# Second MLP: w_out's tiles behind y's second pair, the second maximum behind the turned rows, weights a slot later

## The chip, the cores and the metric

The kernel runs on one core of a Trainium2 chip. Its engines are TensorE (PE in the profile, with its weight loads as PEld), VectorE (DVE), ScalarE (ACT), GpSimd (POOL) and SyncE (SP), which here issues the DMAs. The metric is the device time of one execution in microseconds; the median of three runs stands for the kernel.

## The reference

Three stages in a row: an attention without a score matrix, an MLP, and a second MLP with a softmax and a layer norm in its middle.

```python
q_s = exp(q - max(q, -1));  q_s /= sum(q_s, -1) + 1e-9      # (8, 8, 576, 64)
k_s = exp(k - max(k, 2));   k_s /= sum(k_s, 2) + 1e-9
x = q_s @ (k_s^T @ v)                                       # as 4608 x 512
h = x @ w_in                                                # 512 -> 2048
y = (max(h, 0) + alpha * min(h, 0)) @ w_out                 # 2048 -> 512
h = y @ w_in2                                               # 512 -> 1024
e = exp(h - max(h, -1));  s = h * e / (sum(e, -1) + 1e-9)
ln = (s - mean(s)) / sqrt(var(s) + 1e-6) * g_ln
out = ln @ w_out2                                           # 1024 -> 512
```

## The kernel before

**Products.** Each 2 x 2 block product is done with seven products in place of eight (operands A11, A12, S1 to S4, A22 on one side, B11, B21, T1 to T4, B22 on the other). Each operand is split into a high and a low part (`put`, lines 132 to 134: ACT rounds to the high part, L133, and DVE subtracts it, L134), and each product is three matmuls, high by high, high by low, low by high.

**Stages.** The attention and the first MLP's first pass over nine tiles of 512 tokens (`phase(0)`) end at about 475 us; the second pass (`phase(1)`) runs to about 873 us; then the second MLP goes over 18 pairs of 128-token rows. The weights of the first MLP's second pass are fetched and split during the first pass, in eight slots a tile, from slot 4 of the third last tile on (`z = n - (NTL - 3) * SLOTS - 4`).

**One pair of the second MLP.** `load_y(n)` fetches the seven operands of y from DRAM (y_A, y_S, SP L1372). `pe_h2(n)` makes h in three parts: products into two PSUM banks h2a and h2x, ACT copies a bank that has to be kept (`hold`, r, L1397), DVE adds into hs (L1404, L1412, L1414). `norm_pieces(n, z)` is the softmax and the norm of each of the pair's two 128-token halves z: the maximum on DVE (`top`, L1446), the exponential with its sum on ACT (L1447), `solu` on DVE (L1436 to L1439), squares on ACT (L1449), the variance on DVE (L1442), its root on POOL (L1443), L1451 on DVE, and the scaled rows el on ACT (L1452). `pe_tr(n, z)` turns the rows by TensorE (tp, L1487); ACT copies them (fA, L1498), and DVE and ACT form the operands l and lS of the output product: L1510, L1513, L1515, L1518 and their `put`s; the last row is the low part of S4. `pe_out(n)` makes the output in banks oa and ox, with holds on ACT (or, L1539) and adds on DVE (L1553, L1561, L1563).

**Order.** A scheduler walks the emitted steps by priority and writes one list per engine; an engine does its list in order, and waits where an instruction's inputs aren't there. The loop over pairs emits, for pair n: `pe_h2(n+1, 0)`, `pe_tr(n, 0)`, `pe_h2(n+1, 1)`, `pe_tr(n, 1)`, `norm(n+1, 0)`, `pe_h2(n+1, 2)`, `load_y(n+2)`, `pe_out(n, 0)`, `norm(n+1, 1)`, `pe_out(n, 1)`. `tc.issue_after(x)` ties what is emitted in it behind x in its own engine's list. In pairs 1 to 7 the loop also works off what is left of y: steps `y_late`, which copy and store y's operands (yl, ACT and DVE L133, L134 and SP L529).

**w_out.** Its 14 tiles wo (512 KB each) are fetched by SP at the start of the second MLP: 8 behind y's first pair, in `first_h2`, and 6 behind y's second pair, in `second_h2`.

Of the kernel before, what the change touches and what calls it, by code (L numbers as in the profile page):

```python
# [13 lines left out]
ALU = mybir.AluOpType  # L14
# [6 lines left out]
def attention_then_two_mlps(  # L21
# [42 lines left out]
    NTL = NT // N  # L64
# [41 lines left out]
    def f32(ap):  # L106
        return ap.bitcast(F32)
# [23 lines left out]

    def put(hi, lo, src, eng=V):
        S.activation(hi, src, AF.Copy)  # L133
        eng.tensor_tensor(lo, src, f32(hi), ALU.subtract)  # L134


    wps = [tc.alloc_tile_pool(name="wp0", bufs=7 + FU, side="right")]
# [704 lines left out]
    SLOTS = 8  # L842
# [321 lines left out]
    def hook0(i, s):  # L1164
        n = i * SLOTS + s
        for what in LOADS.get(n, []):
            chunk_load(*what)
        with ExitStack() as behind:
            for ins in booted if i == 0 else ():
                behind.enter_context(tc.issue_after(ins.ins))  # L1170
            for what in READY.get(n, []):
                chunk_ready(*what)
        if (i, s) == SUMS_AT[0]:
            for o in ("S1", "S2", "S3"):
                wc[0, o] = w_tile(0, 0, o)
        if (i, s) in SUMS_AT:
            sums.pop(0)()
        if (i, s) == (TS - 1, 3):
            s4_step(0)
        if (i, s) == (TS, 0):  # L1180
            s4_step(1)
        if (i, s) == (NTL - 3, 4):
            ps_at.release()
            at.release()
            ahead.append(tc.alloc_tile_pool(name="ahead", bufs=1, reuse_waits="tile"))
        z = n - (NTL - 3) * SLOTS - 4
        if 0 <= z < len(NEXT):
            u, o = NEXT[z]
            while to_turn:
                to_turn.pop(0)()  # L1190
            raw = ahead[0].tile([P, N, 2], I32, tag="w64", name=f"a64_{u}_{o}")
            w = ahead[0].tile([P, N], I32, tag="w32", bufs=4 * FU, name=f"a32_{u}_{o}")
            out = not isinstance(o, str)
            src = src_out(1, u, o) if out else src_in(1, u, o)
            load, *turn_ = load_parts(src, raw, w, None if out else 2)
            load()
            to_turn.extend(turn_)
            second[u, o] = f32(w)
        elif z == len(NEXT):
            while to_turn:  # L1200
                to_turn.pop(0)()
        if i == NTL - 1 and s == 2:
            ready["in", 0] = w_in_ops(1, 0, {o: second[0, o] for o in ("A11", "A12", "A21", "A22")}, gp_s(0), V, V)
        if i == NTL - 1 and s in IN_AT:
            for _ in range(IN_AT[s]):
                ready["in", 0].pop(0)()
# [148 lines left out]
    def fetch_wi(o, u):  # L1355
        wi[o] = wps[u].tile([P, 2, N], F32R, tag="w", name=f"wi_{o[0]}_{o[1]}")
        nc.sync.dma_start(out=f32(wi[o]), in_=wi_d[o])

    def fetch_wo(o, pool):
        wo[o] = pool.tile([P, 2, 2, W], F32R, tag="w", bufs=None, name=f"wo_{o[0]}_{o[1]}")  # L1360
        nc.sync.dma_start(out=f32(wo[o]), in_=wo_d[o])
# [3 lines left out]
    def load_y(n):  # L1365


        i, z = divmod(n, 2)
        ys[n] = {}
        for o in STAT:  # L1370
            ys[n][o] = m2["pool"].tile([P, 2, 2, P], F32R, tag=f"y{o}", bufs=1, name=f"y_{n}_{o}")
            asked = nc.sync.dma_start(out=f32(ys[n][o]), in_=y_d[i][STAT.index(o)][:, z])  # L1372
        return asked
# [47 lines left out]
    def norm(n, z):  # L1421
        for piece in norm_pieces(n, z):
            piece()

    def norm_pieces(n, z):
        t = 2 * n + z
        h = hs[n][z]
        st = m2["pool"].tile([P, 8], F32, tag="st", bufs=4, name=f"st_{t}")
        nm, se, rs, su, sq, rstd = (st[:, z:z + 1] for z in range(6))
        if t == 0:  # L1430
            m2["pool"].tile([P, 3 * SHIFT], F32, name="l_edge")
        e = m2["pool"].tile([P, F2], F32, tag="el", bufs=2, name=f"el_{t}")
        lns[t] = e

        def solu():
            V.tensor_scalar_add(se, se, 1e-9)  # L1436
            V.reciprocal(rs, se)
            V.scalar_tensor_tensor(e, h, rs, e, ALU.mult, ALU.mult, accum_out=su)  # L1438
            V.tensor_scalar_mul(su, su, -1.0 / F2)  # L1439

        def spread():
            V.tensor_scalar(sq, sq, 1.0 / F2, 1e-6, ALU.mult, ALU.add)  # L1442
            G.tensor_tensor(rstd, sq, mhalf, ALU.pow)  # L1443

        return [
            lambda: V.tensor_reduce(nm, h, AX.X, ALU.max, negate=True),  # L1446
            lambda: S.activation(e, h, AF.Exp, bias=nm, accum_out=se),  # L1447
            solu,
            lambda: S.activation(h, e, AF.Square, bias=su, accum_out=sq),  # L1449
            spread,  # L1450
            lambda: V.tensor_tensor(su, su, rstd, ALU.mult),  # L1451
            lambda: S.activation(e, e, AF.Identity, bias=su, scale=rstd),  # L1452
        ]
# [18 lines left out]

    def lt_put(n, o, src):
        t = lt_op(n, o)
        put(t[:, 0], t[:, 1], src)

    lf = {}

# [12 lines left out]
    def pe_tr(n, z):  # L1491


        tps = turned_rows(n, z)

        def copy(o, src):
            lf[n, o] = m2["pool"].tile([P, 4, P], F32, tag=f"f{o}", bufs=1, name=f"f{o}_{n}")
            S.activation(lf[n, o], src, AF.Copy)  # L1498

        if z == 0:  # L1500
            copy("A11", tps[0])
            lt_put(n, "A11", tps[0])
            copy("A12", tps[1])
            lt_put(n, "A12", tps[1])
        else:
            copy("A22", tps[1])
            f11, f12, f22 = (lf.pop((n, o)) for o in ("A11", "A12", "A22"))
            t = gp.tile([P, 2, N], F32, tag="rn", bufs=1, name=f"fs_{n}")
            s, s3 = (t[:, y, :].rearrange("p (f q) -> p f q", f=4) for y in range(2))
            V.tensor_tensor(s, tps[0], f22, ALU.add)  # L1510
            a21 = tps[0]
            lt_put(n, "A22", tps[1])
            V.tensor_tensor(s3, f11, a21, ALU.subtract)  # L1513
            lt_put(n, "S1", s)
            V.tensor_tensor(s, s, f11, ALU.subtract)  # L1515
            lt_put(n, "S2", s)
            lt_put(n, "S3", s3)
            V.tensor_tensor(f12, f12, s, ALU.subtract)  # L1518
            lt_put(n, "S4", f12)

    ob = {}

# [87 lines left out]
    def hook1(i, s):  # L1610
        if i == 0:
            hook_w1(i, s)
        if i == 1 and s == 0:
            open_w2()
        if i and s in (4, 5, 6, 0) and y_todo:
            y_todo.pop(0)()
        for step in prep.get((i, s), []):
            step()
        if i == NTL - 1:
            if s in (2, 3):  # L1620
                for o in late[:7][4 * (s - 2):4 * (s - 1)]:
                    fetch_wi(o, 0)
            if s == 7:
                for o in late[7:]:
                    fetch_wi(o, 1)

    def first_h2():
        while y_todo:
            y_todo.pop(0)()
        wr["pool"].release()  # L1630
        xp.release()
        m2["pool"] = tc.alloc_tile_pool(name="m2", bufs=1, reuse_waits="tile")
        m2["pool"].tile([P, STEP], F32, name="y_edge")
        ps_g.release()
        psum["h2"] = tc.alloc_tile_pool(name="ps_h2", bufs=2, space=PSUM, reuse_waits="tile")
        asked = load_y(0)
        m2["w"] = tc.alloc_tile_pool(name="m2w", bufs=2, reuse_waits="tile")
        m2["w"].tile([P, SHIFT], F32, name="w_edge")
        with tc.issue_after(asked.ins):
            for z in range(8):  # L1640
                fetch_wo(WO[z], wps[z // 4])

    def second_h2():
        for z in range(3):
            pe_h2(0, z)
        load_y(1)
        norm(0, 0)
        for z in range(8, 14):
            fetch_wo(WO[z], wps[1] if z < 12 else m2["w"])

    phase(1, [first_h2, second_h2], hook1)
    norm(0, 1)
# [9 lines left out]
    for n in range(NPR - 2):  # L1662
        at_end = pe_h2(n + 1, 0)
        with ExitStack() as behind:
            if n == 0:
                behind.enter_context(tc.issue_after(at_end.ins))
            pe_tr(n, 0)
        if n:
            store_y(asked)
        if n and y_late:  # L1670
            y_late.pop(0)()
        pe_h2(n + 1, 1)
        pe_tr(n, 1)
        norm(n + 1, 0)
        pe_h2(n + 1, 2)
        asked = load_y(n + 2)
        store_y(asked)
        pe_out(n, 0)
        norm(n + 1, 1)
        if n and y_late:  # L1680
            y_late.pop(0)()
        if n < NPR - 3:
            pe_out(n, 1)
# [144 lines left out]
```

## Time and profile before

| | us |
|---|---|
| median of three runs | 1285.52 |
| the three runs | 1282.73 to 1285.69 |
| the profiled execution | 1283.44 |
| its span in the trace | 1281.7 |
| PE busy | 1242.3 (97%) |
| DVE busy | 1009.2 (79%) |
| ACT busy | 792.6 (62%) |

The granted TensorE clock was 0.999 of full speed (2.4 GHz) over the span. A row of the timeline reads: start, duration, engine, line, operation, out <- in, and in brackets the engine's idle time before it with what released it. A busy PE is counted from modelled ends, so the windows below are read by their length first.

### The profile page before, as it was taken

To read this page: it belongs to the slowest core of one execution; us is meant where nothing else is said; L and a number is where in the kernel's file an instruction comes from. 1 tells how busy PE (TensorE), PEld (TensorE's weight loads), DVE (VectorE), ACT (ScalarE), POOL (GpSimd) and SP (SyncE) were. 2 spreads that over 40 slices of the span, in tenths; PEclk is the share of its full clock that TensorE was granted. 3 is DMA by queue.
4 is the path that set the end of the run, shared out by engine and by line. 5 is a ranking of instruction groups with operands and counts; after the bars stand their busy time and mean duration, and the time that the engine had idled before them with its cause. 6 is when DMAs were issued, how large, how long until landed. Compare 5 with 4: busy or idle time off the path is not lost.

```text
span 1281.7 us, 22036 instructions
## 1 busy us (share of the span) xinstructions
PE 1242.3 (97%) x8443; PEld 1109.2 (87%) x8443; DVE 1009.2 (79%) x1818; ACT 792.6 (62%) x1371; POOL 27.0 (2%) x52
## 2 busy tenths in 40 slices
PE   4899999999999999999999999999999999999998
PEld 3788888898988889998998999997888888898988
DVE  7899987988866687887889888864777778686865
ACT  5776554654655565654566555544777677777774
POOL 0100000000000000000000000000000000000000
PEclk9999999999999999999999999999999999999999
DMA  9964553454424430534665557579434345334312
GB/s 242 286 175 137 144 151 105 120 172 104 141 72 146 142 139 33 210 127 177 243 230 209 202 197 263 190 243 379 148 119 150 118 134 154 115 109 112 111 59 50
DMA packets 153401, 203.83 MB, mean 159 GB/s; under 512 B 57144, under 2 KB 105296, under 8 KB 150096
## 3 DMA queue, kind: packets, MB, share of 16 engines
q1 hardware_dynamic: 152208, 201.38, 48.8%
q0 software_dynamic: 1088, 1.05, 0.5%
q8 instruction: 66, 1.08, 0.4%
q14 instruction: 39, 0.32, 0.1%
HBM read 126.37 MB, written 76.02 MB: 158 GB/s over the span
## 4 chain that ended last, share of the span: by engine, by line
PE 77%; DMA 8%; DVE 8%; ACT 5%; issue 1%; SPq 1%; POOL 0%; ACTq 0%; DVEq 0%; POOLq 0%
PE acc L471 8%; PE acc L472 8%; PE acc L473 8%; PE ga L361 4%; PE ga L362 4%; PE ga L363 4%; PE gx L361 3%; PE gx L363 3%; PE gx L362 3%; PE oa L1533 2%; PE tp L1487 2%; PE h2a L1390 2%; PE h2a L1392 2%; PE h2a L1391 2%; PE oa L1534 2%; PE oa L1535 2%
## 5 line engine op out<-in xcount | busy, mean ns | idle before, releaser
L471 PE MATMUL acc<-gg,w 128*128 128x512 f32 x576 | 226.0, 392 | 0.9 <-ACT w L212 0.9
L472 PE MATMUL acc<-gg,w 128*128 128x512 f32 x576 | 226.7, 394 | 0.0
L473 PE MATMUL acc<-gg,w 128*128 128x512 f32 x576 | 224.3, 391 | 0.0
L473 PEld LDWEIGHTS acc<-gg,w 128*128 128x128 f32 x576 | 108.1, 188 | 23.3 <-DVE w L213 0.3
L471 PEld LDWEIGHTS acc<-gg,w 128*128 128x128 f32 x576 | 108.2, 188 | 20.3 <-ACT w L212 1.0
L472 PEld LDWEIGHTS acc<-gg,w 128*128 128x128 f32 x576 | 108.2, 188 | 17.9 <-DVE gg L134 0.3
L134 DVE TENSOR_TENSOR gg<-t,gg 128x1024 fp32r<-128x1024 f32 x72 | 88.0, 1222 | 14.5 <-ACT gg L133 14.4
L133 ACT ACTIVATE gg<-t 128x1024 fp32r<-128x1024 f32 x72 | 76.5, 1063 | 30.0 <-DVE t L452 20.7
L452 DVE SCALAR_TENSOR_TENSOR t<-rn,calpha,t 128x512 f32<-128x512 f32 x120 | 84.7, 748 | 9.2 <-ACT rn L449 9.2
L449 ACT ACTIVATE rn<-t 128x1024 f32<-128x1024 f32 x60 | 63.2, 1053 | 32.4 <-DVE t L438 32.3
L134 DVE TENSOR_TENSOR l<-tp,l 128x512 fp32r<-128x512 f32 x50 | 34.3, 685 | 46.6 <-ACT l L133 46.6
L361 PE MATMUL ga<-xT,w_S 128*128 128x256 f32 x240 | 68.3, 285 | 1.3 <-ACT r L370 1.3
L363 PE MATMUL ga<-xT,w_S 128*128 128x256 f32 x240 | 67.0, 279 | 0.0
L362 PE MATMUL ga<-xT,w_S 128*128 128x256 f32 x240 | 67.0, 279 | 0.0
L370 ACT ACTIVATE r<-ga 128x512 f32<-128x512 f32 x60 | 35.7, 594 | 41.1 <-PE ga L363 40.9
L1452 ACT ACTIVATE el<-el,st 128x1024 f32<-128x1024 f32 x36 | 44.5, 1242 | 21.2 <-DVE st L1451 10.0
L389 PE MATMUL h<-xB,w_c 128*128 128x256 f32 x192 | 54.9, 288 | 1.4 <-ACT w_c L212 1.3
L391 PE MATMUL h<-xB,w_c 128*128 128x256 f32 x192 | 54.7, 285 | 1.1 <-DVE w_c L213 1.0
L390 PE MATMUL h<-xB,w_c 128*128 128x256 f32 x192 | 54.4, 284 | 0.0
L1498 ACT ACTIVATE fA<-tp 128x512 f32<-128x512 f32 x50 | 30.1, 603 | 30.1 <-PE tp L1487 30.1
L361 PEld LDWEIGHTS ga<-xT,w_S 128*128 128x128 f32 x240 | 45.1, 188 | 4.1 <-ACT r L370 2.3
L1438 DVE SCALAR_TENSOR_TENSOR el<-hs,st,el 128x1024 f32<-128x1024 f32 x36 | 46.2, 1282 | 0.6
(399 smaller groups left out, 3990.8 us busy)
## 6 DMA issues: line engine op xcount, KB each, us to landing
y_S<-y_d SPq DMA_DIRECT2D x72, 256.0 KB, 3.0
xraw<-x_d SPq DMA_DIRECT2D x16, 1024.0 KB, 4.9
y_d<-yo_S SPq DMA_DIRECT2D x32, 512.0 KB, 3.5
y_A<-y_d SPq DMA_DIRECT2D x54, 256.0 KB, 2.7
y_d<-yo_A SPq DMA_DIRECT2D x24, 512.0 KB, 2.9
p_d<-pt SPq DMA_DIRECT2D x36, 256.0 KB, 3.5
part<-p_d SPq DMA_DIRECT2D x9, 1024.0 KB, 8.3
q<-in_q_dram SPq DMA_DIRECT2D x16, 512.0 KB, 5.5
```

The source lines that it names most:

```text
L133: S.activation(hi, src, AF.Copy)
L134: eng.tensor_tensor(lo, src, f32(hi), ALU.subtract)
L361: T.matmul(bank[:, z, :], wh, x[:, 0, c, :], start=first and z == 0, stop=False, **go_on)
L362: T.matmul(bank[:, z, :], wh, x[:, 1, c, :], start=False, stop=False, **go_on)
L363: T.matmul(bank[:, z, :], wl, x[:, 0, c, :], start=False, stop=c == 1, **go_on)
L389: T.matmul(out, w[:, 0, c, :], x[:, 0, c % 2, :], start=c == 0 and h == 0, stop=False, **go_on)
L391: T.matmul(out, w[:, 1, c, :], x[:, 0, c % 2, :], start=False, stop=c == KC - 1, **go_on)
L449: S.activation(rn, t, AF.Relu, scale=-1.0)
L452: V.scalar_tensor_tensor(t[:, j, :], rn[:, j, :], calpha[:, fg + j:fg + j + 1], t[:, j, :], ALU.mult, ALU.add)
L471: T.matmul(a, wh, g[:, 0, :], start=u == 0 and f == 0, stop=False)
L472: T.matmul(a, wh, g[:, 1, :], start=False, stop=False)
L473: T.matmul(a, wl, g[:, 0, :], start=False, stop=u == NU - 1 and f == FU - 1)
```

## The change

Four edits. The last maximum of a pair (`top` of `norm(n+1, 1)`) is tied on DVE behind the last row of `pe_tr(n, 1)`, for which `put`, `lt_put` and `pe_tr` return it. Of the wo tiles, 2 are fetched at slot 7 of the last tile of the first MLP, 2 behind y's first pair, and 10 behind y's second pair. The weights of the first MLP's second pass are fetched one slot later, and their pools are released one slot later.

```diff
-        if (i, s) == (NTL - 3, 4):
+        if (i, s) == (NTL - 3, 5):
             ps_at.release()
...
-        z = n - (NTL - 3) * SLOTS - 4
+        z = n - (NTL - 3) * SLOTS - 5
...
             if s == 7:
                 for o in late[7:]:
                     fetch_wi(o, 1)
+                for z in range(2):
+                    fetch_wo(WO[z], wps[0])
...
         with tc.issue_after(asked.ins):
-            for z in range(8):
-                fetch_wo(WO[z], wps[z // 4])
+            for z in range(2, 4):
+                fetch_wo(WO[z], wps[0])
...
-        load_y(1)
+        asked = load_y(1)
         norm(0, 0)
-        for z in range(8, 14):
-            fetch_wo(WO[z], wps[1] if z < 12 else m2["w"])
+        with tc.issue_after(asked.ins):
+            for z in range(4, 14):
+                fetch_wo(WO[z], wps[1] if z < 12 else m2["w"])
...
-        pe_tr(n, 1)
+        turned_all = pe_tr(n, 1)
...
-        norm(n + 1, 1)
+        top, *others = norm_pieces(n + 1, 1)
+        with tc.issue_after(turned_all.ins):
+            top()
+        for piece in others:
+            piece()
```

The first place is DVE's list in pair 9. hs_0 and st_12039 belong to the first half of pair 10, hs_1 and st_12132 to its second half, lS and l are operands of pair 9, and L1446 is the second maximum. Before:

```order
L1446 TENSOR_REDUCE st_12132<-hs_1_11943 128x1
L1515 TENSOR_TENSOR fs_12020<-fs_12020,fA_9_11985 128x512
L134 TENSOR_TENSOR lS_9_12033<-fs_12020,lS_9_12033 128x512
L1518 TENSOR_TENSOR fA_9_11990<-fA_9_11990,fs_12020 128x512
L1437 RECIPROCAL st_12039<-st_12039 128x1
L1553 TENSOR_TENSOR ob_9_12075<-ox_12074,or_9_12089 128x256
L134 TENSOR_TENSOR lS_9_12030<-fs_12020,lS_9_12030 128x512
L1438 SCALAR_TENSOR_TENSOR el_12040,st_12039<-hs_0_11942,st_12039,el_12040 128x1024
L134 TENSOR_TENSOR l_9_12022<-fA_9_11990,l_9_12022 128x512
L1439 TENSOR_SCALAR st_12039<-st_12039 128x1
L1436 TENSOR_SCALAR st_12132<-st_12132 128x1
```

The same place now:

```order
L1518 TENSOR_TENSOR fA_9_11990<-fA_9_11990,fs_12020 128x512
L134 TENSOR_TENSOR lS_9_12030<-fs_12020,lS_9_12030 128x512
L1437 RECIPROCAL st_12039<-st_12039 128x1
L1553 TENSOR_TENSOR ob_9_12075<-ox_12074,or_9_12089 128x256
L134 TENSOR_TENSOR l_9_12022<-fA_9_11990,l_9_12022 128x512
L1438 SCALAR_TENSOR_TENSOR el_12040,st_12039<-hs_0_11942,st_12039,el_12040 128x1024
L1446 TENSOR_REDUCE st_12132<-hs_1_11943 128x1
L1439 TENSOR_SCALAR st_12039<-st_12039 128x1
L1561 TENSOR_TENSOR ob_9_12076<-oa_12073,or_9_12130 128x256
L1436 TENSOR_SCALAR st_12132<-st_12132 128x1
L1437 RECIPROCAL st_12132<-st_12132 128x1
L1438 SCALAR_TENSOR_TENSOR el_12133,st_12132<-hs_1_11943,st_12132,el_12133 128x1024
```

The second maximum went from in front of L1515 to behind S4's low part (l_9 <- fA_9) and behind L1438 of the first half; the second half's L1436, L1437 and L1438 follow it, and the low part of S4 stands in front of the first L1438 now.

The second place is ACT's list in the same pair, from the holds of the output on. el_12040 is the first half of pair 10, el_12133 the second, r_11 are the holds of pair 11. Before:

```order
L1539 ACTIVATE or_9_12116<-oa_12073 128x256
L1449 ACTIVATE hs_0_11942,st_12039<-el_12040,st_12039 128x1024
L1539 ACTIVATE or_9_12130<-ox_12074 128x256
L1452 ACTIVATE el_12040<-el_12040,st_12039 128x1024
L1449 ACTIVATE hs_1_11943,st_12132<-el_12133,st_12132 128x1024
L1566 ACTIVATE ob_9_12076<-oa_12073 128x256
L1452 ACTIVATE el_12133<-el_12133,st_12132 128x1024
L1397 ACTIVATE r_11_12211<-h2a_12186 128x512
L1397 ACTIVATE r_11_12219<-h2x_12187 128x512
```

The same stretch now:

```order
L1539 ACTIVATE or_9_12116<-oa_12073 128x256
L1539 ACTIVATE or_9_12130<-ox_12074 128x256
L1447 ACTIVATE el_12133,st_12132<-hs_1_11943,st_12132 128x1024
L1449 ACTIVATE hs_0_11942,st_12039<-el_12040,st_12039 128x1024
L1452 ACTIVATE el_12040<-el_12040,st_12039 128x1024
L1449 ACTIVATE hs_1_11943,st_12132<-el_12133,st_12132 128x1024
L1566 ACTIVATE ob_9_12076<-oa_12073 128x256
L1397 ACTIVATE r_11_12211<-h2a_12186 128x512
L1452 ACTIVATE el_12133<-el_12133,st_12132 128x1024
L1397 ACTIVATE r_11_12219<-h2x_12187 128x512
```

The second exponential (L1447, in front of this stretch before) stands behind the holds of the output, and one of the two holds r moved in front of the second L1452.

The third place is PE's list in the second pair's h, at the start of the second MLP; h2a and h2x are the two banks, wi_T_1_9187 the end of the operand T2, wi_T_0_9189 and wi_T_1_9191 are T1, wi_T_0_9225 and wi_T_1_9227 T3, and tp the first pair's turned rows. Before:

```order
L1392 MATMUL h2a_9652<-wi_T_1_9187,y_S_9571 128x512
L1390 MATMUL h2x_9653<-wi_T_0_9189,y_S_9573 128x512
L1391 MATMUL h2x_9653<-wi_T_0_9189,y_S_9573 128x512
L1392 MATMUL h2x_9653<-wi_T_0_9189,y_S_9573 128x512
L1390 MATMUL h2x_9653<-wi_T_1_9191,y_S_9573 128x512
L1391 MATMUL h2x_9653<-wi_T_1_9191,y_S_9573 128x512
L1392 MATMUL h2x_9653<-wi_T_1_9191,y_S_9573 128x512
L1487 MATMUL tp_0_0_9687<-ident,el_9583 128x128 x4
L1487 MATMUL tp_0_1_9692<-ident,el_9583 128x128 x4
L1390 MATMUL h2a_9652<-wi_T_0_9225,y_S_9575 128x512
```

The same place now:

```order
L1392 MATMUL h2a_9652<-wi_T_1_9187,y_S_9563 128x512
L1390 MATMUL h2a_9652<-wi_T_0_9225,y_S_9567 128x512
L1391 MATMUL h2a_9652<-wi_T_0_9225,y_S_9567 128x512
L1392 MATMUL h2a_9652<-wi_T_0_9225,y_S_9567 128x512
L1390 MATMUL h2a_9652<-wi_T_1_9227,y_S_9567 128x512
L1390 MATMUL h2x_9653<-wi_T_0_9189,y_S_9565 128x512
```

T3's product into h2a comes right behind T2's now, where the products with T1 into h2x and eight transposes stood between; the hold r of bank h2a (ACT, L1397) lies between the two.

## Rows read from the trace of the kernel before

**Rows 1.** The page: busy us (share of the span) xinstructions.
```profile
PE   1242.3 (97%) x8443; PEld 1109.2 (87%) x8443; DVE 1009.2 (79%) x1818; ACT 792.6 (62%) x1371; POOL 27.0 (2%) x52
```

**Rows 2.** Waits of PE, 840 to 1282 us: total us, times, longest us.
```profile
PE oa L1533 <- ACT lS L133: 3.5, 7, 1.3
PE h2a L1390 <- ACT r L1397: 2.3, 1, 2.3
...
PE h2a L1390 <- DMA y_A<-y_d: 0.6, 1, 0.6
```

**Rows 3.** Windows of 8 and 7 pairs: length, engines' busy us, clock, DMA share, GB/s.
```profile
902.51:1079.87 177.36, 173.56 (x1138) 154.72 (x1137) 133.29 (x286) 129.38 (x238) 8.77 (x16) 1.00 0.43 134
1079.87:1230.39 150.52, 150.52 (x995) 135.62 (x994) 109.48 (x232) 108.77 (x197) 7.68 (x14) 1.00 0.36 111
```

**Rows 4.** Timeline of DVE in one late pair (pair 9): start, duration.
```profile
1140.42 0.69 DVE L134 TENSOR_TENSOR l<-tp,l 128x512 fp32r<-128x512 f32 x1 [3.32 <-ACT l L133]
...
1144.16 0.68 DVE L1510 TENSOR_TENSOR fs<-tp,fA 128x512 f32<-128x512 f32 x1
...
1146.75 1.21 DVE L1446 TENSOR_REDUCE st<-hs 128x1 f32<-128x1024 f32 x1
1147.88 0.68 DVE L1515 TENSOR_TENSOR fs<-fs,fA 128x512 f32<-128x512 f32 x1
...
1151.88 0.69 DVE L134 TENSOR_TENSOR l<-fA,l 128x512 fp32r<-128x512 f32 x1
1152.48 0.15 DVE L1439 TENSOR_SCALAR st<-st 128x1 f32<-128x1 f32 x1
1152.54 0.15 DVE L1436 TENSOR_SCALAR st<-st 128x1 f32<-128x1 f32 x1
...
1154.14 0.15 DVE L1442 TENSOR_SCALAR st<-st 128x1 f32<-128x1 f32 x1
...
1161.90 0.69 DVE L134 TENSOR_TENSOR l<-tp,l 128x512 fp32r<-128x512 f32 x1 [3.31 <-ACT l L133]
```

**Rows 5.** Timeline of ACT in the same pair.
```profile
1143.17 0.60 ACT L1498 ACTIVATE fA<-tp 128x512 f32<-128x512 f32 x1 [1.81 <-PE tp L1487]
...
1148.00 1.16 ACT L1447 ACTIVATE el<-hs,st 128x1024 f32<-128x1024 f32 x1 [0.68 <-DVE st L1446]
1149.06 0.18 ACT L1447 ACTIVATION_READ_ACCUMULATOR el<-hs,st 128x1 f32 x1
...
1155.20 1.24 ACT L1452 ACTIVATE el<-el,st 128x1024 f32<-128x1024 f32 x1 [1.02 <-DVE st L1439]
...
1158.68 1.25 ACT L1452 ACTIVATE el<-el,st 128x1024 f32<-128x1024 f32 x1 [0.84 <-DVE st L1451]
...
1160.31 0.59 ACT L1397 ACTIVATE r<-h2x 128x512 f32<-128x512 f32 x1
1160.79 0.60 ACT L1498 ACTIVATE fA<-tp 128x512 f32<-128x512 f32 x1
```

**Rows 6.** Timeline of ACT in an early pair (pair 4).
```profile
995.65 0.42 ACT L133 ACTIVATE yl_A<-part 128x256 fp32r<-128x256 f32 x1 [1.98 <-DMA y_d<-yl_S]
995.97 1.13 ACT L1447 ACTIVATE el<-hs,st 128x1024 f32<-128x1024 f32 x1
```

**Rows 7.** Timeline of PE in the same pair.
```profile
997.77 0.38 PE L1533 MATMUL oa<-wo_T,lS 128*128 128x256 f32 x1 [1.34 <-ACT lS L133]
```

**Rows 8.** The chain of waits, 865 to 895 us: start, us, what.
```profile
883.91 5.26 DMA y_S<-y_d
...
893.17 0.49 ACT r L1397
...
893.71 0.50 PE h2a L1390
```

**Rows 9.** Waits of PE, 395 to 476 us.
```profile
PE ga L361 <- ACT r L370: 1.3, 4, 0.4
PE ga L361 <- DVE t L436: 1.0, 1, 1.0
```

More of the change, by code (lines that the diff above doesn't have):

```diff
@@ L133, in put @@
         S.activation(hi, src, AF.Copy)
-        eng.tensor_tensor(lo, src, f32(hi), ALU.subtract)
+        return eng.tensor_tensor(lo, src, f32(hi), ALU.subtract)
     wps = [tc.alloc_tile_pool(name="wp0", bufs=7 + FU, side="right")]
@@ L1474, in lt_put @@
         t = lt_op(n, o)
-        put(t[:, 0], t[:, 1], src)
+        return put(t[:, 0], t[:, 1], src)
     lf = {}
@@ L1518, in pe_tr @@
             V.tensor_tensor(f12, f12, s, ALU.subtract)
-            lt_put(n, "S4", f12)
+            return lt_put(n, "S4", f12)
     ob = {}
```

## The prediction, on record before the changed kernel ran

> **What bounds the kernel now.** I read the page first: PE is busy for 97% of the span [rows 1], so a change pays only by what it does to PE's few waits, or by making PE wait elsewhere. Then the waits of PE in the second MLP: 3.5 us in seven waits of an output product for the high part of lS, 2.3 us in one wait for a hold of the second pair's h, and 0.6 us for the first y [rows 2]. Two windows, cut at the starts of the first output product of a pair, show where they lie: eight early pairs take 177.36 us, or 22.17 each, and seven late pairs 150.52 us, or 21.50 each, in which PE is busy for the whole window [rows 3]. So 21.50 is PE's own pace, and the early pairs hold (22.17 - 21.50) x 8 = 5.4 us more than that. The granted clock is 1.00 in both windows, so nothing of this is the clock.
>
> The reader is to look next at how DVE and ACT go through a late pair, since nothing in the sum is as important. DVE begins a pair with the low part of l at 1140.42, behind an idle time, and the next pair with the same step at 1161.90, 21.48 us later [rows 4]. In between the rows form a loop that closes: DVE's list up to 1151.88, the first half's L1452 on ACT at 1155.20, the second half's at 1158.68, fA at 1160.79 [rows 5], and DVE again. PE shows no wait there, yet the loop is as long as PE's pace: the cover for anything that lengthens it is small, and it is used up pair after pair.
>
> **The second maximum in the late pairs.** I set the loop's start to 0 and go through the new list. Before, DVE's list up to the end of the first half's L1438 takes 1151.88 - 1140.42 = 11.46. The maximum leaves that stretch (1147.88 - 1146.75 = 1.13) and S4's low part enters it (1152.48 - 1151.88 = 0.60): 10.93 [rows 4]. Behind it now comes the maximum, whose result is there 1.21 later, at 12.14. The exponential began 0.04 behind the maximum's end (1146.75 + 1.21 = 1147.96, 1148.00) and its sum was there 1.24 later (1149.06 + 0.18) [rows 4, 5]: 13.42. From the second half's L1436 to the first half's L1442 behind it took 1154.14 - 1152.54 = 1.60 on DVE; with 0.04 of latency that is 15.06, where before it was 1154.14 - 1140.42 = 13.72. From that L1442 over POOL to the first L1452 on ACT took 1155.20 - 1154.14 = 1.06: 16.12. From the first L1452 to the second took 3.48: 19.60. From there to fA took 2.11 with two holds r in between; one of them now stands in front of the L1452, in the time in which ACT waits for POOL anyway, so 2.11 - 0.48 = 1.63 (the hold at 1160.31, fA at 1160.79): 21.23. To the next low part took 1161.90 - 1160.79 = 1.11: **22.34, against 21.48 before, or 0.86 us more a pair.**
>
> Not every pair has this list. In every third pair (3, 6, 10, 13) the first half's L1438 stands in front of S4's and S2's low parts, and the first L1452 no longer waits for the second half's L1438; there only the exponential's end, 13.42 on ACT, is in front of it. By the same steps the second L1452 then comes about 0.5 earlier than before, and with the hold gone the loop is about 1.0 shorter, 20.5. Two such loops of 22.34 and one of 20.5 are 65.2 per three pairs, 21.73 each, if the short one makes good what the long ones lost; if PE's pace keeps it from that, a long pair costs its whole 0.86. So a late pair costs between 0.25 and 0.86; I take 0.5, near the middle, because a short pair can give back only what PE lets it. Eight pairs: **+4.0**, from 0 (some slack that the rows don't show) to 6.9 (8 x 0.86).
>
> **The second maximum in the early pairs.** The wait of 1.34 us in pair 4 [rows 7] comes from ACT's list: a step of yl waits 1.98 us for a store until 995.65, and behind it stand the exponential at 995.97 and only then the high part of lS [rows 6]. In the new list the exponential stands behind lS, and S2's high part in front of the first yl, so this wait goes. At first sight that is worth the whole 5.4 us. But the pair then has the loop of the late pairs, between 21.73 and 22.34, with the middle at 22.0, and the second yl step stands between the first half's L1449 and L1452, inside the loop; its place on ACT is 995.97 - 995.65 = 0.32 us, and its store may be late as that of the row was. I take 0.3 for it: 22.3 a pair against 22.17, **+1.0 us** over eight pairs. The ends: -5.4, if PE goes at its own pace, and +4, if half a microsecond of the store's wait falls into every pair.
>
> Here a rule of the Trainium skill speaks for the change. The page "Perfetto Trace Analysis", section "Optimization Strategy", says to look for the gaps of the most contended engine, to see which engine's update ends them, and to let that one finish sooner. By this rule alone the sum of the steady loop would be -5.4. The rows agree that the gap is there and who ends it; what they show besides is that the same two engines close a loop that is as long as PE's pace, so the update can come sooner in one place only by coming later in another.
>
> **The start of the second MLP.** The hold that PE waits for at 893.71 stands at the end of a chain through y's loads: a load of y_S takes 5.26 us from 883.91 on [rows 8]. Those loads of the second pair stood behind eight wo tiles in SP's list and stand behind four now, so they land earlier by up to four tiles' time. I let the 2.3 and the 0.6 us [rows 2] go: -2.9. A new wait takes their place: T3's product into h2a comes directly behind T2's, and between them lies the hold. From the hold's start to PE's start it took 893.71 - 893.17 = 0.54 [rows 8], and PE's pipeline ends a little behind the issue of the next matmul, so at least 0.6; with one row of ACT of 1.24 in front of the hold (as long as an L1452 [rows 5]) it would be 1.9. In pair 0 there is one more: the bank ox must be read by L1553 before the first product with S1 may write it. From fA's start over L1510 to where the maximum stood it took 1146.75 - 1143.17 = 3.6 in the late pair [rows 4, 5], and the new list of PE has some 2.0 us of products between; 1.6 us. I take 0.7 for the first and nothing for the second, since that pair's share of the lS wait goes at the same time (at most 1.3 [rows 2]). **-2.2**, from -2.9 to +0.6. For the ten tiles behind y's second pair I count nothing: that pair lands by 889.2 (883.91 + 5.26) or sooner and the first output product begins at 902.51 [rows 3, 8], so some 13 us cover them; a tile that still lands too late would cost a wait of up to a load's 5 us.
>
> **The weights a slot later.** This moves ACT and DVE rows and DMAs by an eighth of a tile in the last three tiles of the first pass, where PE's waits are 1.3 us for ACT's r and 1.0 us for DVE's t [rows 9]. They may go, or as many may come in another slot. Zero, from -2.3 to +2.3. What `put` returns adds no instruction.
>
> **The sum.** -2.2 + 1.0 + 4.0 + 0 = +2.8. The startup's extra wait in pair 0 may add its 1.6 less 1.3; I add 0.4 and come to +3.2. The profiled execution took 1283.44, so the changed one would take 1286.6; the median of the runs is 2.1 above the profiled execution, which gives 1288.7, and I write **1289 us**, 0.27% slower. What a measurement of this kernel can tell from no change is about 0.3%, 3.9 us, so this forecast lies just inside.
>
> **The rivals.** First, faster: the lS waits go, and the lengthened loop is absorbed because PE's consumers of l and el have slack that the rows of a late pair, in which nothing waits, don't show. Then early pairs fall to 21.50, late ones stay: -5.4 - 2.2 = -7.6, or 1278. For it speaks that late pairs show PE without a wait; against it that slack is used once, not eight times. It decides if a late pair's ACT list still ends in front of PE's turn. The rule cited above would give this result. Second, not slower and not faster: the loop's lengthening is only the 0.25 of the lower bound and the early pairs gain it back (21.8 against 22.17, -3.0, and +2.0 late): -3.2 with the start, within the bound at 1282.3. Third, clearly slower: the second yl step waits in front of the first half's L1452 in every early pair, as the 1.98 us of pair 4 [rows 6] did elsewhere: +4 early, +6.9 late, -1 at the start, +9.9, or 1295. It decides from the store's landing on: if a store lands later than 16 us into the loop, the first L1452 is late by the rest. That the change does not do what it says is excluded by the lists: the maximum stands behind S4's low part in every pair of them.
>
> **How the numbers follow.** The forecast (loop longer by about half a microsecond, +1 to +7) has 0.55, the first rival 0.20, the second 0.13, the third 0.12. Of the forecast's 0.55, 0.25 lie within 0.3% and 0.30 above. The first rival gives 0.17 faster and 0.03 the same, the second 0.03 and 0.10, the third is slower. Faster 0.20, the same 0.38, slower 0.42. The forecast's own range is 1286.5 to 1292.5; to leave out no more than 2 in 10 it has to take in half of the first rival and half of the third: 1281 to 1295.5.
>
> **What would show it.** A late pair of the changed kernel above 21.50 us between the starts of its first output product, with a wait of PE for DVE's or ACT's step of the loop, in two pairs out of three, shows the main term right; late pairs of 21.50 show it wrong. In the early pairs the wait of the output product for lS should be nearly gone; if the period is under 21.8 there, the loop has more slack than I count. At the start the wait of 2.3 us should be gone, and a shorter one for r should stand at T3's first product. The prediction falls if the late pairs keep PE's pace, or if a wait for a store in front of L1452 stands in the early pairs.

## The result and the profile after

The changed kernel took 1295.29 us (median of six runs, 1292.02 to 1296.40), the kernel before on the same chip 1285.38. The ratio is 1.0074, with an interval of 1.0058 to 1.0091: the change makes the kernel slower by 0.74%, or 9.9 us. The forecast was slower by 3.5; the time lies just inside the range's upper end of 1295.5, where the third rival stood.

The waits of PE in the second MLP of the changed kernel (840 to 1295 us: total us, times, longest us) answer to [rows 2]:

```profile
PE tp L1487 <- DVE l L134: 3.9, 13, 0.6
PE h2x L1390 <- DVE hs L1404: 3.0, 3, 2.1
PE ox L1533 <- DVE ob L1553: 2.1, 1, 2.1
PE h2a L1390 <- ACT r L1397: 0.7, 1, 0.7
```

The waits for lS (3.5 us) are gone, and the wait for the hold r has gone from 2.3 to 0.7 us. In their place PE waits 13 times for a low part of l before it may turn the second half's rows (before 2 times, 0.6 us), a wait for L1553 stands in pair 0, and there are three waits for L1404, the longest, 2.11 us, in the last pair of the table below (before one, 0.4 us). The windows, cut at the same starts of an output product as [rows 3], show the pairs (length, then busy us of PE, PEld, DVE, ACT, POOL, clock, DMA share, GB/s):

```profile
902.92:1086.21 183.29, 177.04 (x1145) 154.16 (x1144) 135.26 (x289) 133.51 (x241) 9.52 (x16) 1.00 0.44 141
1086.21:1241.95 155.74, 153.91 (x995) 133.97 (x994) 109.81 (x232) 110.10 (x196) 7.70 (x14) 1.00 0.36 107
```

The seven late pairs take 22.25 us each instead of 21.50, at the same granted clock of 1.00 and with the same number of DVE rows (232). The table puts the whole second MLP together for the two profiled executions. The first column's mark is one matmul near the end of the first MLP (847.65 in before, 851.30 after); the starts of a pair's first output product cut the rest.

| us | mark to pair 0 | pair 0 | pairs 1-7 | pairs 8-14 | pair 15 | end |
|---|---|---|---|---|---|---|
| before | 54.86 | 22.22 | 155.14 | 150.52 | 24.87 | 26.44 |
| after | 51.62 | 26.07 | 157.22 | 155.74 | 26.27 | 26.38 |
| difference | -3.24 | +3.85 | +2.08 | +5.22 | +1.40 | -0.06 |

The sum is +9.25, close to the 9.9 of the medians. The profiled executions differ by 12.9 us of span; the other 3.65 lie ahead of the mark. Two versions below have the same program there and their marks differ by 3.1 us, so 3.65 us there is about what two executions of one program differ by; that the change has no part in it is not shown by these two profiles alone, and the third experiment bears on it.

The loop of the prediction can be checked step by step in a late pair with the long list, the turn of pair 11. (Pairs are counted here by their first output products, from 0; by this count the pair of [rows 4, 5], called pair 9 there, is also pair 11.) First DVE, start and duration:

```profile
1149.09 0.69 DVE L134 TENSOR_TENSOR l<-tp,l 128x512 fp32r<-128x512 f32 x1 [2.83 <-ACT l L133]
...
1158.80 1.28 DVE L1438 SCALAR_TENSOR_TENSOR el<-hs,st,el 128x1024 f32<-128x1024 f32 x1
...
1160.01 1.22 DVE L1446 TENSOR_REDUCE st<-hs 128x1 f32<-128x1024 f32 x1
...
1163.04 1.28 DVE L1438 SCALAR_TENSOR_TENSOR el<-hs,st,el 128x1024 f32<-128x1024 f32 x1
...
1164.25 0.15 DVE L1442 TENSOR_SCALAR st<-st 128x1 f32<-128x1 f32 x1
...
1171.53 0.69 DVE L134 TENSOR_TENSOR l<-tp,l 128x512 fp32r<-128x512 f32 x1 [2.83 <-ACT l L133]
```

Then ACT in the same pair:

```profile
1161.32 1.16 ACT L1447 ACTIVATE el<-hs,st 128x1024 f32<-128x1024 f32 x1
...
1165.32 1.25 ACT L1452 ACTIVATE el<-el,st 128x1024 f32<-128x1024 f32 x1 [1.62 <-DVE st L1439]
...
1168.80 1.25 ACT L1452 ACTIVATE el<-el,st 128x1024 f32<-128x1024 f32 x1 [0.35 <-DVE st L1451]
...
1170.42 0.59 ACT L1498 ACTIVATE fA<-tp 128x512 f32<-128x512 f32 x1
```

Counted from 1149.09, the maximum is there at 12.14 (predicted 12.14), L1442 begins at 15.16 (15.06), the first L1452 at 16.23 (16.12), the second at 19.71 (19.60), fA at 21.33 (21.23), and the loop closes at 22.44 (22.34). Against [rows 4, 5] every step behind the maximum is late. Where PE feels it is the next row of the loop:

```profile
1150.30 0.68 DVE L134 TENSOR_TENSOR l<-tp,l 128x512 fp32r<-128x512 f32 x1
...
1151.13 0.63 PE L1487 MATMUL tp<-ident,el 128*128 128x128 f32 x4 [0.31 <-DVE l L134]
```

PE may write the second half's turned rows only when the low part has read the bank, 1150.30 + 0.68; the wait that is shown is only 0.31 of the pair's loss. The starts show more. Now, around the second half's transposes:

```profile
1150.22 0.60 PE L1487 MATMUL tp<-ident,el 128*128 128x128 f32 x4
...
1151.51 0.48 PE L1390 MATMUL h2a<-wi_T,y_A 128*128 128x512 f32 x1
```

The same place before:

```profile
1142.10 1.03 PE L1487 MATMUL tp<-ident,el 128*128 128x128 f32 x8
1142.89 0.49 PE L1390 MATMUL h2a<-wi_T,y_A 128*128 128x512 f32 x1
```

From the transposes to the next product it takes 1.29 us, before 0.79. PE counts as busy in part of it (153.91 in the window, 150.52 before), since its matmuls' ends are modelled.

### The profile page after: what moved, and what is told of

The parts are those of the page before. It is cut to its first block, busy times and chain, and to the rows that moved or that the text cites. A ratio compares the mean times of both kernels' runs of the same rounds, so it can differ in the third digit from the quotient of the medians.

```text
span 1294.6 us, 22041 instructions
## 1 busy us (share of the span) xinstructions
PE 1248.9 (96%) x8443; PEld 1107.4 (86%) x8443; DVE 1009.6 (78%) x1818; ACT 796.4 (62%) x1371; POOL 27.8 (2%) x52
## 4 chain that ended last, share of the span: by engine, by line
PE 67%; DVE 15%; ACT 8%; DMA 6%; issue 2%; POOL 1%; SPq 0%; ACTq 0%; DVEq 0%; POOLq 0%
PE acc L471 8%; PE acc L472 8%; PE acc L473 8%; PE ga L361 3%; PE ga L363 3%; PE ga L362 3%; PE gx L361 3%; PE gx L363 2%; PE gx L362 2%; ACT el L1452 2%; PE oa L1533 2%; PE h L391 2%; PE h L389 2%; PE h L390 2%; PE oa L1535 2%
## 5 line engine op out<-in xcount | busy, mean ns | idle before, releaser
L1452 ACT ACTIVATE el<-el,st 128x1024 f32<-128x1024 f32 x36 | 44.7, 1243 | 26.0 <-DVE st L1439 15.4
L1438 DVE SCALAR_TENSOR_TENSOR el<-hs,st,el 128x1024 f32<-128x1024 f32 x36 | 46.2, 1282 | 0.7
L1443 POOL TENSOR_TENSOR st<-st,mhalf 128x1 f32<-128x1 f32 x36 | 20.5, 570 | 1216.0 <-DVE st L1442 1216.0
```

## The experiments

In all of them the kernel before ran on the same chip; a ratio is against it, and the line numbers of a version may be a few off. A first set takes the edits one by one.

**The tie alone.** Of the change's diff only the lines of `put`, `lt_put`, `pe_tr` and `top`.

> Only the tie of the second maximum; w_out's loads and the weights' slot as before. Theory (the tie lengthens the loop of DVE and ACT): the late pairs take 22.2 us instead of 21.50 (+0.75 x 8 = +6), pairs 1 to 7 together about +2, the start as before with PE's wait of 2.3 us for the hold, the stretch to 873 us as before; together +7 to +8.5 us. Rival (the late pairs are longer because of what the moved w_out loads or the moved weights do to memory or to the buffers): late pairs stay at 21.50 and the whole is within 2 us of before.

Measured: 1295.05 us, ratio 1.0083 (1.0070 to 1.0097). Its windows:

```profile
902.86:1082.74 179.88, 175.35 (x1137) 153.27 (x1136) 133.23 (x286) 131.86 (x238) 8.99 (x16) 1.00 0.43 132
1082.74:1238.49 155.75, 153.97 (x995) 134.05 (x994) 109.75 (x232) 110.06 (x196) 7.67 (x14) 1.00 0.35 107
```

Late pairs 155.75, to 0.01 us as in the changed kernel (155.74). This stretch hardly scatters: in four executions without the tie (the kernel before, the next two versions, and the one without the hold below) it takes 150.45 to 150.52. The tie explains the late pairs wholly, and by itself costs as much as the whole change. Pair 0 takes 23.40, 1.2 more than before, pairs 1 to 7 1.3 more (less than that stretch scatters by, as the third run shows), and the last pair 2.0 more. The total was expected 2 to 4 us lower; what was missed are pair 0 and the last pair.

**w_out's loads alone.** Of the diff only `hook1`, `first_h2` and `second_h2`.

> Only w_out's loads moved. Theory: the second MLP's first output product comes 3 us sooner, because y's second pair lands sooner; the late pairs stay at 21.50, and pair 0 has no wait of 2 us for L1553, since four products of h stand in front of the first product with S1 here; -2 to -3 us. Rival (the wait for L1553 in pair 0 comes from the moved loads by themselves): pair 0 takes 26 us here too, and the whole is 0 to +1 us.

Measured: 1286.08 us, ratio 1.0016 (1.0007 to 1.0024), slower by 2 us: a miss. From the mark to pair 0 it takes 51.64, 3.2 us less (expected 3), but pair 0 takes 25.06 (before 22.22). PE's waits in its early pairs (902 to 1082 us):

```profile
PE oa L1533 <- ACT lS L133: 4.6, 7, 1.8
PE ox L1533 <- DVE ob L1553: 1.6, 1, 1.6
PE h2a L1390 <- DMA y_A<-y_d: 0.5, 1, 0.5
```

So the wait for L1553 in pair 0 comes with the loads, and the tie is not needed for it: the rival was right in this, though it put the whole at 0 to +1 us. Start and pair 0 together come to -0.4; the rest of the 2 us is not placed. Pairs 1 to 7 take 156.26 here, but that stretch scatters, as the next run shows. The late pairs stay at 150.45.

**The weights alone, a slot later.** Of the diff only the two lines with `NTL - 3`.

> Only the first MLP's weights a slot later. Theory: PE's waits between 395 and 476 us grow by 2 us as they did in the changed kernel (0.8 for L428, more for r), nothing else moves: +1.5 to +2.5 us. Rival (the 2 us there are the scatter between two executions): within 0.7 us of before in that stretch.

Measured: 1285.14 us, ratio 1.0006 (0.9997 to 1.0015), no difference. PE's waits from 395 to 476 us are

```profile
PE ga L361 <- ACT r L370: 0.9, 2, 0.6
PE ga L361 <- DVE t L436: 0.7, 1, 0.7
PE gx L361 <- DVE t L428: 0.4, 2, 0.3
```

2.0 us in all, where [rows 9] have 2.3 and the changed kernel had 3.7. The rival holds: what is seen there in one execution is scatter.

The same profile shows another scatter. Its engines' lists in pairs 1 to 7 are those of the kernel before, yet these pairs take 157.81 us instead of 155.14, and more than in the changed kernel (157.22). In pair 4 the yl step waits longer for its store, and PE after it:

```profile
997.96 0.42 ACT L133 ACTIVATE yl_A<-part 128x256 fp32r<-128x256 f32 x1 [3.10 <-DMA y_d<-yl_S]
```

[rows 6] have 1.98 us for it.

A second set asks whether the loop of DVE and ACT is the cause of the long pairs. From pair 9 on a row of the loop is left out, with the tie and without it. These three versions ran once each, and their late windows are read from the trace.

```diff
-            hb[n].append(hold(bx, 5))
+            hb[n].append(hold(bx, 5) if n < 9 else hb[n][2])
```

**The tie, without the hold r5.**

> The tie alone, and from pair 9 on the hold r5 of bank h2x (the last hold in front of fA on ACT, 0.48 us) is left out; the kept hold r2 is read in its place, so a part of h is not computed. Theory (the late pairs are bound by the loop through this ACT row): the late pairs go from 22.2 to 21.75 us. Rival (they are bound by something that is not on this loop, such as the turned rows' bank or the loads): they stay at 22.2.

Measured in the late window:

```profile
1085.28:1238.81 153.53, 151.58 (x995) 134.53 (x994) 109.71 (x232) 107.31 (x190) 7.67 (x14) 1.00 0.36 109
```

21.93 us a pair, 0.32 less than with the tie alone. The direction is the theory's, and "stays at 22.2" is out. The mean was expected at 21.75. From low part to low part a long list falls from 22.4 to 21.9, the whole 0.48; but without the hold every late pair gets the long list, and the short one (21.9 with the hold) no longer occurs.

**The kernel before, without the hold r5.**

> The kernel before without the hold r5 of bank h2x from pair 9 on (the kept hold r2 is read in its place, so a part of h is not computed). Theory (without the tie the late pairs are bound by PE): late pairs stay at 21.50. Rival (they are bound by the loop over DVE and ACT even before): they fall by up to 0.48.

Measured: the late window is 150.51, as before (150.52). Without the tie the same row of ACT is worth nothing: PE is the bound.

**The tie, with one maximum for both halves.**

```diff
+        one_max = z == 1 and 9 <= n < NPR - 2
+        if one_max:
+            nm = firsts[n]
...
-            lambda: V.tensor_reduce(nm, h, AX.X, ALU.max, negate=True),
+            (lambda: None) if one_max else lambda: V.tensor_reduce(nm, h, AX.X, ALU.max, negate=True),
```

> The tie alone, and from pair 9 on the second half's maximum is left out (the first half's is used for both, which leaves the function of the exponential but not its shift). Theory (what costs is the place of this one DVE row in the loop): late pairs go back from 22.2 to PE's 21.5. Rival (the cost is that S2's and S4's low parts come sooner and collide with other rows): they stay above 22.

Measured in the late window:

```profile
1082.02:1232.29 150.27, 150.27 (x996) 135.42 (x995) 103.08 (x225) 109.76 (x197) 7.67 (x14) 1.00 0.37 111
```

Seven DVE rows fewer (225 against 232), one in each pair, and the pairs are at PE's pace again, 21.47. In this kernel nothing is tied in the late pairs any more, and S2's and S4's low parts also stand elsewhere, so it shows that the maximum in its new place is needed for the loss, and not that every part of the 0.75 is its 1.13 us.

A third set goes after the early pairs' 5.4 us by another way than the change.

**yl behind S2's high part.** No maximum is moved. The pair's first yl step, whose wait for a store stood in front of lS [rows 6, 7], is tied behind S2's high part on ACT.

```diff
-        if n and y_late:
-            y_late.pop(0)()
         pe_h2(n + 1, 1)
-        pe_tr(n, 1)
+        high = pe_tr(n, 1)
+        if n and y_late:
+            with tc.issue_after(high.ins):
+                y_late.pop(0)()
```

> The kernel before, with one change: in pairs 1 to 7 the first step of yl is tied on ACT behind the high part of S2, so that its wait for a store (1.98 us in pair 4 of before) no longer stands in front of lS. Theory (the early pairs' 5.4 us come from that ACT row, not from the maximum): the waits of the output product for lS in pairs 1 to 7 are gone, the pairs take 21.6 us instead of 22.1 and the whole is 2 to 4 us faster. Rival (the early pairs are bound by the added DVE and ACT work of yl itself, wherever it stands): pairs 1 to 7 stay at 22.1, within 1 us of before.

Measured: 1283.01 us, ratio 0.9986 (0.9973 to 0.9999), 1.9 us faster where 2 to 4 were expected. Pairs 1 to 7 take 152.89 instead of 155.14, below the four executions without the tie and with this step in its old place (154.58 to 157.81); five of the seven take 21.44 to 21.55. Its waits of PE in the early pairs:

```profile
PE oa L1535 <- DVE ob L1563: 1.2, 2, 0.8
PE oa L1535 <- ACT lS L133: 0.6, 1, 0.6
```

The waits for lS are down to one, in pair 0. What keeps two pairs long is a new one, for an output add.

**The same with w_out's loads moved.**

> The same, with w_out's loads moved as in the changed kernel. Theory (the start's gain of 3 us is lost again in pair 0, because PE gets ahead of a first pair whose norm is not ready sooner): first output product 3 us sooner, pair 0 at 25 us, whole within 1 us of the run without the moved loads. Rival (the gain was lost to the yl steps that follow): 2 us faster than without the moved loads.

Measured: 1281.41 us, ratio 0.9973 (0.9959 to 0.9987), 1.6 us below the run without the moved loads, but the two intervals overlap. By the traces mark to pair 0 is 51.42 (53.71 without) and pair 0 is 25.04 (22.23): the start's gain is given back in pair 0, as the theory says, to within 0.6 us. The medians stand between the theory's 1 us and the rival's 2; what they differ by is open.

**The second yl step behind the output's add.** In the trace of that run PE waits 1.44 us for L1563 in pair 2; this add is L1561 of the kernel before, since the lines here lie two further on. DVE in front of it:

```profile
960.06 0.43 DVE L134 TENSOR_TENSOR yl_S<-part,yl_S 128x256 fp32r<-128x256 f32 x1 [1.62 <-ACT yl_S L133]
960.40 0.15 DVE L1452 TENSOR_TENSOR st<-st 128x1 f32<-128x1 f32 x1
960.47 0.15 DVE L1440 TENSOR_SCALAR st<-st 128x1 f32<-128x1 f32 x1
960.54 0.41 DVE L1563 TENSOR_TENSOR ob<-oa,or 128x256 f32<-128x256 f32 x1
```

DVE stands idle for 1.62 us in front of yl's low part. The step goes behind the add that comes next (L1565 here, L1563 before), and so behind this one too:

```diff
-        if n and y_late:
-            y_late.pop(0)()
         if n < NPR - 3:
-            pe_out(n, 1)
+            added = pe_out(n, 1)
+        if n and y_late:
+            with tc.issue_after(added.ins):
+                y_late.pop(0)()
```

> The kernel with the first yl step behind S2 and w_out's loads moved, and the pair's second yl step tied on DVE behind the output's add L1563 (here L1565). Theory (the two waits of PE for that add, 1.4 and 0.3 us in pairs 2 and 6, come from the yl rows in front of it): both go, pairs 2 and 6 take 21.6 instead of 23.5 and 22.4, whole 1.5 to 3 us faster than without this tie, about 1279. Rival (the early pairs that are long are those in which a store lands late): pairs 2 and 6 stay long.

Measured: 1280.12 us, ratio 0.9970 (0.9959 to 0.9981). The 1.5 to 3 us against the version in front of it don't show in the medians (0.9973 there, on another chip); they show in the traces. Every pair from 1 to 14 takes 21.46 to 21.59, and pairs 1 to 7 take 150.77 together, 2.7 us less than in the version in front of it and 4.4 us less than before. Its windows:

```profile
899.62:1075.49 175.87, 173.82 (x1145) 155.91 (x1144) 135.48 (x290) 131.54 (x242) 9.94 (x16) 1.00 0.45 142
1075.49:1226.02 150.53, 150.53 (x995) 135.60 (x994) 109.43 (x232) 108.78 (x197) 7.70 (x14) 1.00 0.39 119
```

This version beats both kernels. What is left over PE's pace in its first window lies in pair 0 (25.10), where PE waits 1.3 us for a load of y (y_A) and 0.7 us for L1555, the L1553 of the kernel before; the load's wait is not followed further here.

**Pair 0's L1438 behind the first add.** The next pair's L1438 is emitted behind `pe_out(0, 0)` and tied behind its first add.

> The same, and in pair 0 the next pair's L1438 is tied behind the output's first add L1553 (here L1555). Theory (pair 0's wait of 1.7 us is that add, held up by L1438 of 1.28 us and a put): pair 0 goes from 25.0 to 23.5 us. Rival (the wait stands for the first pair's norm, which comes no sooner than before; PE, now ahead, waits for the next row of the same chain): a wait for lS takes its place and pair 0 stays at 25.

Measured: 1279.87 us, ratio 0.9963 (0.9952 to 0.9975), not to be told from the version in front of it. Pair 0 takes 26.20, not 23.5, and PE waits there for something else:

```profile
PE ox L1535 <- ACT lS L133: 1.7, 1, 1.7
```

The wait for the add is gone and one for lS stands in its place: the rival holds, but for the pair's length, which grew by 1.1 us and did not stay. PE is ahead there, and the next row of the first pair's own chain is what it meets.

## Why the prediction was right, and where not

**The direction and its cause** were right: the loop of DVE and ACT, as long as PE's pace before, becomes longer with the maximum behind S4's low part. The tie alone reproduces the late pairs to 0.01 us, leaving the maximum out brings them back to 21.47, and leaving a hold of the same loop out helps with the tie (0.32 us a pair) and not without it (150.51 against 150.52 over seven pairs). That the time came out inside the stated range is luck: it lies above the forecast's own range, 1286.5 to 1292.5, and only 0.2 us below the end at 1295.5, which was put there to take in half of the third rival.

**The late pairs' size** was off: +4.0 for eight pairs was forecast, and +5.22 for seven and +1.40 for the last were measured, 6.6 in all. The long list was worked out to 0.1 us (22.34, measured 22.44). The last pair's 1.40 goes with PE's wait for L1404 (2.11, before 0.40), a row that DVE now does behind the moved maximum (starts 1253.45 and 1249.20). The step that failed is the one on every third pair: "the loop is about 1.0 shorter, 20.5", able to give back what the long pairs lost. From low part to low part the short pairs take 21.92 (1127.17 to 1149.09, the turn of pair 10). The maximum and the two L1452 in it:

```profile
1138.93 1.21 DVE L1446 TENSOR_REDUCE st<-hs 128x1 f32<-128x1024 f32 x1
...
1141.40 1.23 ACT L1452 ACTIVATE el<-el,st 128x1024 f32<-128x1024 f32 x1
...
1146.36 1.25 ACT L1452 ACTIVATE el<-el,st 128x1024 f32<-128x1024 f32 x1 [0.35 <-DVE st L1451]
```

The first L1452 comes at 14.23, earlier than before (14.78 by [rows 4, 5]), as was said. But from it to the second takes 4.96 us and not the 3.48 of the long list, since the second half's own chain starts from the late maximum here too; the second L1452 stands at 19.19, where the prediction has it about 0.5 earlier than before (18.26). 21.92 is still above PE's 21.50, so nothing is given back; the mean is (22.44 + 22.41 + 21.92) / 3 = 22.26, the 22.25 of the window. The bound of 0.86 a pair (6.9) was nearly the whole truth.

**The early pairs** were forecast +1.0 over eight. The waits for lS did go, as said, and pairs 1 to 7 did not get shorter for it. That they got longer is not shown: the two profiles differ by +2.08, but without the tie four executions take 154.58 to 157.81 there and with it four take 156.22 to 157.22. In the changed kernel pairs 1 and 4 are longer from low part to low part (22.97 and 23.46) than the long list is in pairs 2 and 5 (22.57 and 22.56). In both a yl step now waits for a store inside the loop:

```profile
941.54 0.42 ACT L133 ACTIVATE yl_A<-part 128x256 fp32r<-128x256 f32 x1 [1.85 <-DMA y_d<-yl_A]
941.86 1.23 ACT L1452 ACTIVATE el<-el,st 128x1024 f32<-128x1024 f32 x1
...
1001.44 0.42 ACT L133 ACTIVATE yl_A<-part 128x256 fp32r<-128x256 f32 x1 [1.55 <-DMA y_d<-yl_S]
1001.76 0.62 ACT L133 ACTIVATE l<-fA 128x512 fp32r<-128x512 f32 x1
```

In pair 1 it is the second step in front of the first L1452, which the prediction named as a sign against itself; in pair 4 it is the first step, in front of S4's high part. The cause of the wait for lS was named rightly (a yl step on ACT in front of lS); the version that moves this step and not the maximum shows it, with 2.25 us won in the same pairs. The Trainium skill's page "Perfetto Trace Analysis", section "Optimization Strategy", cited in the prediction, says to let what ends the gaps start sooner or finish faster. In this case it came out where the row that was moved itself waited: tying yl, which waited 1.98 us for a store, shortens the pairs, and moving the maximum, which waited for nothing, does not.

**Pair 0** is the term that was mis-sized most: +3.85, for which the prediction had 0.4 (its own 1.6 less 1.3 is 0.3). It named the wait for L1553 and its 1.6 us (measured 2.14), and then set it off against the lS wait of the same pair and left out that the tie lengthens pair 0 as well (1.2 alone, by the first experiment).

**The start** was -2.2, measured -3.24 from the mark on; the new wait for r was 0.74, predicted 0.7. But the moved loads alone end 2 us slower and not faster: in the trace the gain is paid in pair 0 (+2.84). The -2.2 would have had to be taken together with pair 0, as one term of about zero.

**The weights a slot later** were put at zero, and they are (1.0006, 0.9997 to 1.0015).

**The rivals.** The first, faster by slack that the rows don't show, is out: late pairs lose 0.75 each from the first to the last. The second had the lower bound of 0.25 for a late pair and is out too. The third has the right size mostly for another reason: its late term, 6.9, is what came. Its second yl step in front of the first L1452 waits for a store in pair 1 alone and not in every early pair, and it can't be the main cause, since the late pairs, which have no yl, lose most; its +4 early came as +2.08, and its -1 at the start as +0.6 with pair 0.

## What to carry to other kernels

When a row is moved out of the way of one consumer, follow its own consumers around to where the list begins again: if that loop is as long as the bound engine's pace, the row's time comes back in every round, however small the wait it ends. Where two engines' lists close such a loop, take the length of each kind of list by itself, and do not let a shorter one repay a longer one unless its rows are shown to be earlier. And of a wait ask what the row in front of the late one waited for: the row to move is the one that itself stands idle, here a copy waiting for its buffer's store.

## What the runs showed that was not expected

The stretch ahead of the second MLP scatters by some 3 us between executions of the same program (marks at 848.25 and 851.38 in two versions with the same instructions there), with single waits that come and go, and the early pairs, whose yl steps wait for stores, by up to 2.7 us (155.14 and 157.81 with the same lists); so one profile cannot place a change of 2 us in either. The late pairs repeat to 0.1 us. And a lead of 2.3 to 3.2 us at the start of the second MLP was worth nothing in the traces, three times over: pair 0 gave it back. PE meets the first pair's chain on DVE and ACT there, and the one row that was moved out of its way showed the next one.
